# A bias table spread by one fp32 product, a later start for the third batch's v, and a new table of due times in an attention and feed-forward kernel

## The chip, the cores and the metric

The kernel runs on one core of one Trainium2 chip. The metric is the device time of one execution in microseconds (us). Before the change it is 368.13 us, the median of six runs (367.08 to 368.78).

The engines are named as in the profile: PE is TensorE (PEld its weight loads, which overlap its products), DVE is VectorE, ACT is ScalarE, POOL is GpSimd, SP is SyncE. SP, ACT and POOL issue the DMAs; the DMAs that POOL issues share one queue (q0 in the profile).

## The reference

Eight batches of eight heads of attention over 576 positions, head size 64, with an additive bias that depends on the distance of query and key, are followed by a feed-forward layer with a squared relu:

```
scores = q k^T / 8 + bias_table[bucket(|i - j|)]      # 32 buckets, 8 heads
attn   = softmax(scores);  x = attn v                 # -> 4608 tokens x 512
out    = (relu(x w_in)^2) w_out                       # w_in 512x2048, w_out 2048x512
```

From a distance of 128 on, the bucket is always the last, 31.

## The kernel before

**Attention.** A pair is two heads of one batch; there are 32 pairs, four to a batch. q and k of a pair are loaded (and cast to fp16 by the load), turned so that the head size lies on the partitions, multiplied into PSUM (`st`), raised to exponentials by ACT (`pt` for the first 512 keys, `pm` for the last 64), multiplied by the band of bias factors on DVE (L713), and multiplied by v (`va`, `vm`; L739, L746). For the pairs of batches 0 and 1 (0 to 7) PE turns q and k (L930); from batch 2 on DMA transposes that SP issues do it (L913). Batch 0 is worked in two halves (L812, L835, L857); the later batches whole (L974, L1025, L1000). The scores L812 and L974 use 64 rows of the array, all else 96 or 128.

**Bias.** Since the softmax does not change when one number is added to a whole row, the kernel uses exp(bias - bias of bucket 31), which is 1 from distance 128 on: only a band needs a factor. At the start it makes a table of these factors: `bt_sb` holds the bias table four times over (128 partitions x 8), by a load whose source has a first step of 0 (L376 to L380); `far_sb` holds the last row (L381); a product of a row of ones with `far_sb` (L402) puts that row on all 128 partitions; DVE subtracts (L408); ACT takes the exponential (`ex_sb`, L412); DVE spreads it over four selectors (`eb_sb`, L416); 96 products with one-hot columns (L429) and six copies (L441 on ACT, L443 on DVE) make the table `tb_sb`. It also makes `tm_sb` (L450).

**Feed-forward.** Tokens go in nine groups of 512. First layer: L1442 for group 0 (sixteen blocks of eight products: two halves of the tokens by eight blocks u of w_in; block u needs the piece u//2 of w_in), L1489 for the others, L1373 for parts of groups 7 and 8 in a scheme with seven products for eight. ACT takes the relu (L1452, L1518) and DVE the square. Second layer: L1218, the seven-product scheme with sums of `g` made on DVE (L1173) and sums of w_out made on DVE (L1148).

**Loads.** Issued by POOL in one queue: q and k of every pair, v of batches 0 and 1, w_in and w_out in four pieces each. POOL has eight slots (`r_lane`) for loads under way, so the ninth load is issued only when the first has landed. v of batches 2 to 7 is loaded as fp32 by SP into two rooms (`fs`) and cast by POOL (L630), five loads to a batch. For batch 2 these loads are held: POOL writes one column of each room (L602) and so the SP loads wait for it, and these two writes depend on the issue of the last piece of w_out (`i_wout[-1]`).

**What sets the order.** Every piece of work is an `Op` with costs on its possible engines, dependences, buffers and a due time. `Plan.schedule` walks through time: on each engine it takes, of the ops that can start first, the one with the smallest due time. The order found is written out and kept. `DUES` overwrites the due times of a few hundred ops by number; any change in the number of ops renumbers them.

Of the kernel before, what the change touches and what calls it, by code (L numbers as in the profile page):

```python
# [10 lines left out]
FP32 = mybir.dt.float32  # L11
FP16 = mybir.dt.float16
EXPF = mybir.ActivationFunctionType.Exp
# [5 lines left out]
B, H, S, D = 8, 8, 576, 64  # L19
NP = 4 * B  # L20
NBK = 32
# [20 lines left out]
V_EARLY, V_HW = 18900.0, 2  # L42
LATE2 = 7000
UNITS = {7: 1, 8: 2}
HALVES, HSTEP, HL1 = 1, 1650.0, (20000.0, 34000.0)

AT = (0, 0.5, 2, 2.5, 4, 5.5, 7)
# [15 lines left out]


DUES = """
8:-10082 18:14645 30:300187 31:89669 35:262867 36:167639 40:141372 70:12863 74:14200 76:7923 78:10303 80:10916
82:15510 86:16712 88:11688 90:22888 92:15486 98:18218 100:20325 102:18698 104:24117 106:22274 108:21955
110:20585 112:17720 114:22660 116:24333 118:24854 122:29293 124:30437 126:25266 128:33174 130:36581 132:40609
134:51257 136:44653 138:51581 140:48951 142:50028 144:58149 148:57611 150:61477 152:63431 154:61931 156:66311
158:66889 162:65338 164:65793 166:56376 168:67962 170:72120 172:69290 174:54109 176:67502 178:55993 196:79426  # L70
200:89582 204:93757 206:79008 208:72409 210:77212 214:73183 216:70645 218:79313 220:76603 222:85357 224:89011
226:93142 228:96877 232:85822 234:80876 238:92290 242:97174 244:85699 250:80035 259:178052 260:99215 262:99267
263:94523 265:102830 266:94655 268:90726 272:227849 274:97337 280:99383 284:102139 290:112200 294:119768
298:215875 300:111243 308:120928 316:292455 328:222317 340:120614 352:126648 372:290882 378:160123 388:315874
398:154756 400:154629 416:167698 428:163098 430:170467 446:157625 448:164616 474:193249 476:326588 532:43262
533:37155 566:352427 572:24133 585:21449 586:16465 587:204708 592:14599 602:18206 603:302815 606:16687 614:60883
624:23940 626:227369 635:24572 644:28677 645:32201 647:27594 652:32977 656:87863 662:27958 665:28412 667:205250
672:32876 673:30127 677:28664 678:35226 680:77471 688:28429 694:37858 696:40059 700:223775 702:35900 705:35909
708:53117 711:51743 714:57293 717:49012 723:57165 726:56821 729:45894 730:329911 732:52147 738:53922 741:160549
747:289501 748:55406 753:34997 766:39647 777:43315 780:28378 781:28998 794:190499 796:202913 801:53249 802:51377  # L80
808:35893 816:51696 822:366600 836:39718 838:41544 844:109201 849:53420 855:303647 858:55989 861:68919 874:85061
878:80108 894:83592 903:-31482 937:74470 948:83167 966:71026 967:67606 970:76116 972:74373 981:80209 995:78757
996:75913 997:79135 998:80070 999:81174 1013:88709 1034:85463 1045:100670 1048:345957 1050:105533 1063:95906
1087:126025 1091:130523 1094:105159 1096:130379 1100:125464 1107:123396 1110:104747 1111:120415 1116:126120
1120:119481 1123:112853 1128:107993 1136:132690 1140:133810 1143:114832 1147:125053 1150:33103 1151:132743
1158:127267 1161:133598 1178:111838 1183:122064 1212:107705 1215:110106 1220:108322 1231:116331 1243:107673
1244:132705 1249:136498 1250:141722 1252:138524 1266:154614 1279:137235 1290:170196 1295:139537 1309:155745
1313:157461 1318:142698 1320:168920 1324:178100 1338:169961 1342:165042 1347:151660 1349:165027 1353:178415
1360:154230 1363:160171 1364:172948 1367:167075 1371:182965 1374:172802 1377:182632 1379:188184 1382:183106
1393:150398 1396:136398 1398:139207 1407:162688 1439:159540 1442:165094 1444:160584 1457:156356 1462:162464  # L90
1476:171086 1494:178379 1496:95372 1513:192466 1517:206296 1522:201376 1526:211713 1533:196911 1537:195555
1542:191208 1546:222801 1551:200739 1554:200330 1555:209260 1558:35935 1562:223609 1566:193792 1573:210925
1577:216395 1580:214153 1584:204761 1587:221397 1611:179949 1617:185925 1632:157584 1638:187538 1643:188360
1673:204800 1678:201325 1684:208836 1735:235958 1746:247083 1749:236476 1753:241073 1755:232100 1758:46037
1759:255485 1762:69543 1764:28189 1767:246028 1768:258643 1775:224057 1779:236350 1786:235146 1790:231994
1793:247653 1797:260512 1800:225461 1819:215217 1833:222890 1851:236098 1856:236742 1859:216367 1883:242173
1886:229387 1888:224088 1897:252176 1943:260458 1947:277224 1948:272952 1952:266739 1959:262017 1963:176155
1968:269668 1972:265265 1981:279144 1988:265160 1992:64741 2003:269548 2010:73825 2013:261781 2032:291907
2035:289013 2037:286903 2040:293047 2064:272647 2065:274014 2069:249841 2083:15939 2096:275485 2104:257599
2111:304149 2133:278142 2142:287353 2147:290118 2158:278558 2181:2037 2182:291375 2189:39576 2193:314013  # L100
2198:26159 2207:312042 2222:313361 2229:315890 2233:58447 2240:320979 2243:310630 2258:242331 2260:323734
2267:332321 2280:282131 2283:327244 2285:319375 2290:184346 2296:334274 2333:323519 2354:325059
"""


# [156 lines left out]
def kernel(  # L262
# [10 lines left out]
    nc = tc.nc  # L273
    assert (_bucket(np.arange(128, S)) == NBK - 1).all()

    def io(ins):
        tc.keep_in_program_order(ins)
        return ins
# [3 lines left out]
        oh[i, _bucket(np.abs(252 + i - np.arange(512))), np.arange(512)] = 1.0  # L282
    oh_d = nc.inline_tensor(oh.reshape(128, 512), name="c_oh")
    sel = np.kron(np.eye(4), np.ones((NBK, H))).astype(np.float16)
    id_d = nc.inline_tensor(np.concatenate([np.eye(128, dtype=np.float16), sel], axis=1), name="c_id")

    single = ctx.enter_context(tc.tile_pool(name="single", bufs=1))
# [2 lines left out]
    def sb(name, shape, dtype=FP16):  # L290
        return single.tile(shape, dtype, name=name)
# [4 lines left out]
    w_out_sb = sb("w_out_sb", [128, 16, 512])  # L296
    tb_sb = sb("tb_sb", [128, H, 384])
    tm_sb = sb("tm_sb", [128, 4, 192])
    bt_sb = sb("bt_sb", [128, 8], FP32)
    far_sb = sb("far_sb", [1, 8], FP32)  # L300
    ex_sb = sb("ex_sb", [128, 8])
    eb_sb = sb("eb_sb", [128, 4, 8])
    stg = [[sb(f"{n}s{i}", [128, 12 * D]) for n in "qk"] for i in range(NSTG)]
# [13 lines left out]
    gs = [sb(f"g{i}", [128, 16, GT]) for i in range(NGB)]  # L317

    oh_sb = gs[0][:, 0, :]
    one_sb = gs[0].bitcast(FP32)[0:1, 2, 0:128]  # L320
    fs = [sb(f"f32{i}", [128, 512], FP32) for i in range(NF)]
    rts = [sb(f"rt{i}", [128, GT]) for i in range(NRT)]
    ys = [sb(f"y{i}", [128, 512], FP32) for i in range(NY)]
# [4 lines left out]
    g_ps = [psum.tile([128, 512], FP32, name=f"f{i}") for i in range(3)]  # L328

    P = Plan()  # L330
# [28 lines left out]
    def const(f):  # L359
        return lambda: f  # L360

    def load(*args, **kw):
        return loader(*args, **kw)[0]
# [3 lines left out]
    b_stg = [Buf(r_stg) for _ in range(4 * B)]  # L367
# [5 lines left out]
        for w, (n, e, t) in enumerate((("SP", nc.sync, q), ("ACT", nc.scalar, k)))  # L373
    ]
    l_id = load("SP", nc.sync, const(idsel_sb), const(id_d.ap()), (128, 27), due=-1)
    l_bt = load(  # L376
        "ACT", nc.scalar, const(bt_sb),
        const(bass.AP(tensor=bias_table.tensor, offset=bias_table.offset, ap=[[0, 4]] + [list(x) for x in bias_table.ap])),
        (128, 230), due=0,
    )  # L380
    l_far = load("ACT", nc.scalar, const(far_sb), const(bias_table[NBK - 1 : NBK, :]), (1, 27), due=1)  # L381
    l_oh = load("SP", nc.sync, const(oh_sb), const(oh_d.ap()), (128, 60), due=4)
    tabs = list(hw_specs.get_activation_tables(nc.m.arch))
    P.add(
# [10 lines left out]
        ),  # L395
        due=5,
    )
    z_one = P.add({"DVE": 141.0}, lambda: io(nc.vector.memset(one_sb, 1.0)), due=-2)
    far_b = Buf(r_g)
    o_far = P.add(  # L400
        {"PE": 250.0},
        lambda: io(nc.tensor.matmul(g_ps[far_b.slot][:, 0:8], one_sb, far_sb, start=True, stop=True)),  # L402
        [l_far, z_one], [far_b], 0.0, 0.0, "f",
    )
    o_bt = P.add(
        {"DVE": 150.0},
        lambda: io(
            nc.vector.tensor_tensor(out=bt_sb, in0=bt_sb, in1=g_ps[far_b.slot][:, 0:8], op=mybir.AluOpType.subtract)  # L408
        ),
        [l_bt, o_far], [far_b], -1.0,  # L410
    )
    o_ex = P.add({"ACT": 220.0}, lambda: io(nc.scalar.activation(out=ex_sb, in_=bt_sb, func=EXPF)), [o_bt])  # L412
    o_eb = P.add(
        {"DVE": 230.0},
        lambda: io(
# [89 lines left out]
    def pdue():  # L505
        pool_due[0] += 1.0
        return pool_due[0]
# [21 lines left out]
    def load_rows(p, w):  # L529

        b, hp = divmod(p, 4)
        src = (q, k)[w][b, 2 * hp : 2 * hp + 2]
        l_qk[p, w] = [
            load(
                "POOL", nc.gpsimd,
                lambda e=e: rows(stg[b_stg[p].slot][w])[:, 0:4, ds(64 * e, D)],
                const(src[e, 0:512, :].rearrange("(t p) d -> p t d", p=128)),
                (512, 14.5), s_fix, [b_stg[p]], pdue(),
            )
            for e in range(2)  # L540
        ] + [
            load(
                "POOL", nc.gpsimd,
                lambda: stg[b_stg[p].slot][w][0:64, 512:640].rearrange("p (e d) -> p e d", e=2),
                const(src[:, 512:S, :].rearrange("e p d -> p e d")),
                (128, 14.5), s_fix, [b_stg[p]], pdue(),
            )
        ]

    def cast_first(w):  # L550

# [39 lines left out]
        load_v_tail(b)  # L591

    r_f = Ring(NF, True)

    def load_v_fp32(b):

# [2 lines left out]
        if b == V_HW:  # L599

            held = [
                P.add({"POOL": 60.0}, lambda t=t: io(nc.gpsimd.memset(t[:, 0:1], 0.0)), [i_wout[-1]], (), due)  # L602
                for t in fs
            ]
        for tt in range(5):
# [991 lines left out]
```

## Time and profile before

| | |
|---|---|
| median of six runs | 368.13 us (367.08 to 368.78) |
| the profiled execution's own time | 368.39 us |
| its span, first to last instruction | 366.6 us, so 1.8 us lie around it |
| PE busy | 354.6 us, 97% of the span |
| DVE, ACT, POOL busy | 271.5, 263.1, 186.1 us |
| DMA | 44.28 MB, mean 121 GB/s |
| granted PE clock | 1.00 over nearly the whole span |

The page gives each engine's busy time, then the span in 40 slices with busy tenths. The waits tell which engine waited for whom; the timeline lists instructions with start, duration, engine, line, tiles and, in brackets, the idle time before them. A landing time below is the issue's start in the timeline plus the issue-to-landing time of the DMA list. For the loads around the weights that gives, numbered in the order of the queue: second piece of w_in 33.1 (issued 25.2, 7.9 to landing), a k, the fourth piece of v of batch 1 at 34.7 (26.6 + 8.1), first piece of w_out 38.3, a k, second of w_out 42.1, third of w_in 45.5, third of w_out 48.8 (30.3 + 18.5), fourth of w_in 52.2, fourth of w_out 54.9. The first two loads of v of batch 2 are issued by SP at 35.8 and 36.3 and land 11.9 and 18.0 us later.

### The profile page before, as it was taken

To read this page: it belongs to the slowest core of one execution; us is meant where nothing else is said; L and a number is where in the kernel's file an instruction comes from. 1 tells how busy PE (TensorE), PEld (TensorE's weight loads), DVE (VectorE), ACT (ScalarE), POOL (GpSimd) and SP (SyncE) were. 2 spreads that over 40 slices of the span, in tenths; PEclk is the share of its full clock that TensorE was granted. 3 is DMA by queue.
4 is the path that set the end of the run, shared out by engine and by line. 5 is a ranking of instruction groups with operands and counts; after the bars stand their busy time and mean duration, and the time that the engine had idled before them with its cause. 6 is when DMAs were issued, how large, how long until landed. Compare 5 with 4: busy or idle time off the path is not lost.

```text
span 366.6 us, 10230 instructions
## 1 busy us (share of the span) xinstructions
PE 354.6 (97%) x4062; PEld 253.5 (69%) x4062; DVE 271.5 (74%) x622; ACT 263.1 (72%) x390; POOL 186.1 (51%) x342
## 2 busy tenths in 40 slices
PE   4998999999999999999999999999999999999996
PEld 2767787866378546877776666476667786787785
DVE  3798899957885679477597588756688885787673
ACT  5999998479975888678986778967778434725620
POOL 7987529989999977888777772021000000000000
PEclk9999999999999999999999999999999999999999
DMA  9999999999999999999999996143200232020132
GB/s 162 132 156 175 199 172 121 157 184 181 157 137 160 185 160 188 160 164 168 167 116 161 174 150 99 30 108 84 75 3 13 60 84 64 2 89 0 35 111 88
DMA packets 162294, 44.28 MB, mean 121 GB/s; under 512 B 145734, under 2 KB 162246, under 8 KB 162246
## 3 DMA queue, kind: packets, MB, share of 16 engines
q0 software_dynamic: 74208, 14.53, 52.1%
q1 hardware_dynamic: 87696, 28.80, 43.2%
q8 instruction: 32, 0.52, 0.6%
q10 hardware_dynamic: 342, 0.30, 0.3%
q14 instruction: 16, 0.13, 0.1%
HBM read 36.88 MB, written 9.44 MB: 126 GB/s over the span
## 4 chain that ended last, share of the span: by engine, by line
PE 80%; DMA 7%; DVE 6%; POOL 3%; ACT 2%; issue 1%; POOLq 0%
PE f L1218 27%; PE f L1489 27%; PE pv L746 8%; PE st L974 7%; DMA w_out_sb<-in_moe_w_out_dram 3%; PE pv L739 2%; DMA w_in_sb<-in_moe_w_in_dram 2%; PE f L1442 2%; DMA qs<-in_q_dram 2%; PE st L1025 2%; DVE pt L713 2%; PE st L1000 1%; DVE s L1173 1%; PE st L1373 1%; POOL va L346 1%
## 5 line engine op out<-in xcount | busy, mean ns | idle before, releaser
L987 ACT ACTIVATE pt<-st 128x1024 f16<-128x1024 f32 x112 | 108.8, 1029 | 27.1 <-PE st L974 26.5
L1489 PE MATMUL f<-xt,w_in_sb 128*128 128x512 f16 (+4 forms) x592 | 111.8, 333 | 0.0
L1518 ACT ACTIVATE rt<-f 128x512 f16<-128x512 f32 x116 | 67.8, 607 | 25.8 <-PE f L1489 24.4
L1489 PEld LDWEIGHTS <-w_in_sb 128*128 128x128 f16 x592 | 51.7, 98 | 43.4 <-issue 9.3
L713 DVE TENSOR_TENSOR pt<-pt,tb_sb 128x512 f16<-128x512 f16 (+3 forms) x108 | 62.0, 593 | 12.7 <-ACT pt L987 11.8
L1528 DVE TENSOR_TENSOR g<-rt 128x512 f16<-128x512 f16 x116 | 49.9, 437 | 23.4 <-ACT rt L1518 22.0
L1218 PEld LDWEIGHTS <-g 128*128 128x128 f16 x576 | 54.4, 98 | 9.2 <-issue 2.5
L346 POOL DMA_DIRECT2D ks<-in_k_dram x79 | 55.6, 713 | 6.7 <-DMA w_out_sb<-in_moe_w_out_dram 4.3
L346 POOL DMA_DIRECT2D qs<-in_q_dram x79 | 55.3, 709 | 7.2 <-DMA w_in_sb<-in_moe_w_in_dram 2.8
L746 PE MATMUL pv<-va,pt 128*128 128x65 f16 x1280 | 55.0, 193 | 0.2 <-DVE pt L713 0.2
L746 PEld LDWEIGHTS <-pt 128*128 128x128 f16 x1280 | 50.3, 97 | 2.5 <-DVE pt L713 0.4
L1218 PEld LDWEIGHTS <-s 128*128 128x128 f16 x432 | 41.5, 98 | 8.3 <-issue 2.1
L1246 DVE SCALAR_TENSOR_TENSOR y<-f,y 128x512 f32<-128x512 f32 (+1 forms) x47 | 31.3, 667 | 19.4 <-PE f L1218 16.7
L1218 PE MATMUL f<-wt,g 128*128 128x256 f16 x288 | 36.4, 273 | 0.0
L1218 PE MATMUL f<-w_out_sb,s 128*128 128x256 f16 x288 | 36.2, 273 | 0.0
L739 PE MATMUL pv<-vm,pm 128*128 128x130 f16 x160 | 35.4, 221 | 0.1
L974 PE MATMUL st<-qt,kt 64*128 64x512 f16 x224 | 33.9, 381 | 0.0
L957 POOL COPY qz<-qt 64x64 f16<-64x64 f16 x54 | 18.6, 345 | 29.9 <-DMA qt<-qs 12.6
L1218 PE MATMUL f<-w_out_sb,g 128*128 128x256 f16 x272 | 33.6, 273 | 0.0
L765 DVE TENSOR_TENSOR x<-pv,r 128x384 f16<-128x384 f32 (+1 forms) x64 | 31.2, 488 | 1.3
L1173 DVE TENSOR_TENSOR s<-g,s 128x1024 f16<-128x1024 f16 x36 | 24.8, 692 | 0.2
L760 DVE RECIPROCAL r<-pv 128x6 f32<-128x6 f32 (+1 forms) x64 | 11.9, 186 | 16.9 <-PE pv L746 16.2
(104 smaller groups left out, 422.4 us busy)
## 6 DMA issues: line engine op xcount, KB each, us to landing
out_dram<-y SPq DMA_DIRECT2D x34, 256.0 KB, 2.7
f<-in_v_dram SPq DMA_DIRECT2D x24, 256.0 KB, 5.8
qs<-in_q_dram POOLq DMA_DIRECT2D x48, 64.0 KB, 4.9
ks<-in_k_dram POOLq DMA_DIRECT2D x48, 64.0 KB, 4.6
w_in_sb<-in_moe_w_in_dram POOLq DMA_DIRECT2D x4, 512.0 KB, 11.9
w_out_sb<-in_moe_w_out_dram POOLq DMA_DIRECT2D x4, 512.0 KB, 15.9
qs<-in_q_dram POOLq DMA_DIRECT2D x7, 144.0 KB, 5.1
ks<-in_k_dram POOLq DMA_DIRECT2D x7, 144.0 KB, 5.6
```

Source lines behind the costliest of these rows:

```text
L346: lambda: io(eng.dma_start(out=out_(), in_=in_())),
L713: io(nc.vector.tensor_tensor(out=a, in0=a, in1=t, op=MULT))
L739: nc.tensor.matmul(ps[:, i, :, :], pm[:, c : c + 128], vm[:, hp, :, 0:65], start=True, stop=False)
L746: nc.tensor.matmul(ps[:, i, e, :], pt[:, (2 * jt + e) * S + c : (2 * jt + e) * S + c + 128], va[:, jt, 2 * hp + e, 0:65], start=False, sto ...
L765: nc.vector.tensor_tensor(out=xs[xb.slot][:, qt0 : qt0 + nq, :].rearrange("p t (e d) -> p t e d", e=2), in0=ps[:, :, :, 0:64], in1=rs[rb.s ...
L974: nc.tensor.matmul(sets_ps[st.slot][:, e, :], kt[rw, ts(jt, 128)], qt[rw, 0:512], start=True, stop=True,)
L987: nc.scalar.activation(out=p5(pts[pb.slot])[:, jt, :, 0:512], in_=sets_ps[st.slot], func=EXPF, scale=SCALE)
L1218: nc.tensor.matmul(home[bf.slot][:, ts(s_, HALF)], left(c, s_), right(c), start=(c == 0 and (s_ == 0 or apart) and (own or i not in before ...
L1246: nc.vector.scalar_tensor_tensor(out=dst, in0=ps, scalar=OSC, in1=ys[y[plus].slot][:, cs], op0=MULT, op1=mybir.AluOpType.add,)
L1489: nc.tensor.matmul(g_ps[bank.slot][:, a:z], w_in_sb[:, kk, ts(nt, 128)], xt_sb[:, kk, c : c + z - a], start=(kk == 0), stop=(kk == 3),)
L1518: io(nc.scalar.activation(out=rts[rb.slot], in_=g_ps[bank.slot], func=RELUF))
L1528: nc.vector.tensor_tensor(out=gs[gb1.slot][:, nt, :], in0=rts[rb.slot], in1=rts[rb.slot], op=MULT)
```

## The change

1. The bias table is loaded once, 32 partitions x 8, and the load of its last row goes. A constant `c_rep` (32 x 128, fp32: the identity four times side by side, less 1 in its last row) is loaded in its stead. One fp32 product of the two, over 32 rows, gives on 128 partitions bias - bias of bucket 31; ACT takes the exponential straight from PSUM. The row of ones, the fp32 product over one row and the DVE subtraction go. Both new loads lie in `g0`, in places that `g` uses only later.
2. The two POOL writes that hold v of batch 2 depend on the last issue of pair 8's k (`i_qk[8, 1]`) in place of the last issue of w_out.
3. `DUES` is new throughout. With it the order of all engines changes.

```diff
-8:-10082 18:14645 30:300187 31:89669 35:262867 36:167639 40:141372 70:12863 74:14200 76:7923 78:10303 80:10916
...
+0:6314 10:217026 16:13035 20:13348 21:258484 25:16976 56:-3806 60:10549 64:7807 66:10391 72:10797 74:9599
...
+V_AFTER = 8
...
+    rep = np.tile(np.eye(NBK, dtype=np.float32), (1, 4))
+    rep[NBK - 1] -= 1.0
+    rep_d = nc.inline_tensor(rep, name="c_rep")
...
-    one_sb = gs[0].bitcast(FP32)[0:1, 2, 0:128]
+    rep_sb, bt_sb = (gs[0].bitcast(FP32)[0:NBK, 2 + i, 0:n] for i, n in enumerate((128, H)))
...
-    l_bt = load(
-        "ACT", nc.scalar, const(bt_sb),
-        const(bass.AP(tensor=bias_table.tensor, offset=bias_table.offset, ap=[[0, 4]] + [list(x) for x in bias_table.ap])),
-        (128, 230), due=0,
-    )
-    l_far = load("ACT", nc.scalar, const(far_sb), const(bias_table[NBK - 1 : NBK, :]), (1, 27), due=1)
+    l_bt = load("ACT", nc.scalar, const(bt_sb), const(bias_table), (NBK, 230), due=0)
+    l_rep = load("ACT", nc.scalar, const(rep_sb), const(rep_d.ap()), (NBK, 40), due=1)
...
-    z_one = P.add({"DVE": 141.0}, lambda: io(nc.vector.memset(one_sb, 1.0)), due=-2)
...
     o_far = P.add(
-        {"PE": 250.0},
-        lambda: io(nc.tensor.matmul(g_ps[far_b.slot][:, 0:8], one_sb, far_sb, start=True, stop=True)),
-        [l_far, z_one], [far_b], 0.0, 0.0, "f",
+        {"PE": 560.0},
+        lambda: io(nc.tensor.matmul(g_ps[far_b.slot][:, 0:8], rep_sb, bt_sb, start=True, stop=True)),
+        [l_bt, l_rep], [far_b], 0.0, 0.0, "f",
     )
-    o_bt = P.add(
-        {"DVE": 150.0},
-        lambda: io(
-            nc.vector.tensor_tensor(out=bt_sb, in0=bt_sb, in1=g_ps[far_b.slot][:, 0:8], op=mybir.AluOpType.subtract)
-        ),
-        [l_bt, o_far], [far_b], -1.0,
+    o_ex = P.add(
+        {"ACT": 220.0},
+        lambda: io(nc.scalar.activation(out=ex_sb, in_=g_ps[far_b.slot][:, 0:8], func=EXPF)),
+        [o_far], [far_b],
     )
-    o_ex = P.add({"ACT": 220.0}, lambda: io(nc.scalar.activation(out=ex_sb, in_=bt_sb, func=EXPF)), [o_bt])
...
-                P.add({"POOL": 60.0}, lambda t=t: io(nc.gpsimd.memset(t[:, 0:1], 0.0)), [i_wout[-1]], (), due)
+                P.add({"POOL": 60.0}, lambda t=t: io(nc.gpsimd.memset(t[:, 0:1], 0.0)), [i_qk[V_AFTER, 1]], (), due)
```

The order that results, as far as the prediction uses it. SP issues the constants before the first q, ACT issues the first k as its first load. The cast of the first q moves from ACT to DVE. PE begins with the turns of pair 0's k, then the fp32 product, then pair 0's q, pair 1's k, the first sixteen products of the table, pair 1's q, and only then the first scores. The loads of POOL before the second piece of w_in are the same in number and size; after it come two k, the first piece of w_out, the third of w_in, two pieces of w_out, the fourth piece of v of batch 1, the fourth piece of w_in, the fourth of w_out. The two writes that hold v of batch 2 stand thirteen entries later, behind eight loads of pairs 8 to 10.

## Prediction

> **What bounds the kernel now.** First the busy times and the busy tenths of the page: PE is the engine to watch.
>
> ```profile
> PE 354.6 (97%) x4062; PEld 253.5 (69%) x4062; DVE 271.5 (74%) x622; ACT 263.1 (72%) x390; POOL 186.1 (51%) x342
> ```
>
> Then the busy times by stretch (columns: length, then busy us and count for PE, PEld, DVE, ACT, POOL, then granted clock, DMA share, GB/s), which tell where PE's idle time lies:
>
> ```profile
> 0.00:5.00 5.00, 0.57 (x4) 0.51 (x4) 2.33 (x13) 2.13 (x2) 3.89 (x10) 1.00 0.66 161
> 5.00:10.00 5.00, 4.00 (x58) 2.67 (x59) 1.06 (x7) 3.98 (x8) 4.11 (x8) 1.00 1.58 162
> 10.00:20.00 10.00, 8.66 (x208) 6.25 (x208) 8.09 (x25) 9.86 (x17) 9.22 (x16) 1.00 1.28 134
> 20.00:30.00 10.00, 9.50 (x185) 6.83 (x182) 9.39 (x30) 10.00 (x16) 9.06 (x14) 1.00 1.51 153
> 30.00:40.00 10.00, 8.85 (x152) 6.75 (x149) 7.04 (x25) 9.04 (x15) 6.40 (x21) 1.00 1.33 194
> 40.00:50.00 10.00, 9.83 (x140) 8.05 (x138) 9.74 (x28) 9.15 (x14) 4.80 (x8) 1.00 1.22 196
> 50.00:100.00 50.00, 49.76 (x550) 33.74 (x549) 41.22 (x89) 40.24 (x61) 43.76 (x74) 1.00 1.60 159
> 100.00:200.00 100.00, 99.91 (x1176) 71.41 (x1176) 72.83 (x159) 78.27 (x112) 85.25 (x153) 1.00 1.50 161
> ```
>
> From 50 us on PE is idle for 0.3 us in 150, later for nothing; before 50 us it is idle 8.6 us, 5.4 of them in the first 10. Between 10 and 30 us ACT is full (19.86 of 20). So after 50 us the time is PE's work; only the first 50 us can give anything back. Last the waits of PE between 4 and 60 us and the timeline at the two places that matter below:
>
> ```profile
> PE f L930 <- ACT qs L555: 2.4, 1, 2.4
> PE f L930 <- DMA ks<-in_k_dram: 1.0, 1, 1.0
> PE f L835 <- POOL qz L957: 0.8, 1, 0.8
> ...
> 33.85 0.45 PE L930 MATMUL f<-id_sb,ks 96*64 96x96 f16 x12 [0.98 <-DMA ks<-in_k_dram]
> ...
> 42.93 0.22 PE L739 MATMUL pv<-vm,pm 128*128 128x130 f16 x1
> ```
>
> The first wait is the start itself (first data, first cast). The one at 33.85 is for the k of a pair of batch 1. At 42.93 the first values of pair 4 begin: eight us after the last piece of their v landed (34.7), so that load is far from the path now.
>
> **Work after 50 us.** The change leaves PE's products the same in kind and number but for the fp32 one. Each visit to the 64-row scores costs PE a turn there and back: after L974 the next group starts 0.54 us later (34.48 to 35.02) where 2 x 0.21 would do. In the built order those turns number 112 before and after for L974, so this term is 0. For the early L812 they go from 24 to 28: two more visits, at some 0.15 to 0.3 us a turn **+0.6** (0 if they fall into ACT's full stretch, 1.2 at most).
>
> **The first 10 us.** This is the old chain of the table in the timeline:
>
> ```profile
> 2.06 0.56 PE L402 MATMUL f<-far_sb,g 1*128 1x8 f32 x2 [2.06 <-DMA far_sb<-in_bias_table_dram]
> 4.10 0.84 ACT L555 ACTIVATE qs<-g 96x768 f16<-96x768 f32 x1 [0.46 <-DMA g<-in_q_dram]
> 5.22 0.84 ACT L555 ACTIVATE ks<-g 96x768 f16<-96x768 f32 x1 [0.28 <-DMA g<-in_k_dram]
> 8.82 0.16 DVE L408 TENSOR_TENSOR bt_sb<-bt_sb,f 128x8 f32<-128x8 f32 x1
> 9.51 0.20 ACT L412 ACTIVATE ex_sb<-bt_sb 128x8 f16<-128x8 f32 x1
> 9.75 0.18 DVE L416 TENSOR_TENSOR eb_sb<-id_sb,ex_sb 128x32 f16<-128x32 f16 x1 [0.77 <-ACT ex_sb L412]
> ```
>
> L408 (0.16) and the memset (0.17) go; both lay in idle DVE time (3.4 of 10 us busy), so they give 0. The load of 128 rows of 32 B goes: 4 KB among 2.27 MB of the first 15 us, 0 in transfer, and its 0.64 us of issue on ACT ended at 2.3, before ACT's first cast could start; its successor takes as long or less. Now the k is issued at 0.74 as q was, so it should land at 4.1 and be cast on ACT to 4.9; its turns on PE run 5.0 to 5.7 (0.69 each, as the row of L930 at 4.99 has it). The fp32 product comes next; the trace shows it over one row only, 0.56. Over 32 rows I take 0.56 (0.35 if only one of the two passes counts, 1.4 if like a turn of twelve it doubles). PE then waits for the q cast, now on DVE: no such cast is in the trace; the nearest DVE row, fp32 from PSUM, 128x512 (L443), is 0.645, so 0.97 for 768, and fp16 rows at 0.44 per 512 give 0.65. I take 0.8: q lands at 5.2, is cast by 6.0, while the fp32 product ends at 6.3. Exponential 6.5, selectors 6.9, table products from about 8.0, two us before the old 9.97. But the order puts these ahead of the first scores: pair 0's go from 7.94 to about 9.2 and ACT's first big exponential from 8.60 to about 10.3. Early table, late scores: by 10 us PE has done 48 turns either way. **0** (-0.4 to +0.8).
>
> The Trainium skill has a rule on this cast, "VectorE: DVE Perf Modes": a copy with one fp32 source in SBUF runs at twice the rate, as it takes both read ports. By it the cast would be about 0.45 us, an estimate from the page's rates; no row here shows it, and the sum stays the same since the fp32 product ends later anyway.
>
> **ACT's full stretch, 10 to 34 us.** Up to the last exponential of batch 0 ACT loses the q cast (0.84), two turned copies (2 x 0.6) and one table copy (0.62), 2.6 us; it gains 1.5 to 2.2 of idle time before 16 us, as its exponentials start late and wait for table products between them. **-0.4** (-1.1 to +0.3).
>
> **The wait at 33.85.** In the new order three turns stand together, but five further L1442 blocks, one more turn of twelve, and one more half of scores stand ahead of pair 4's values. PE reaches the awaited k later than it lands (33.8): **-1.0** (0 if the pair before it is late).
>
> **What is late next: v of batch 1.** Its fourth piece now lies behind two k, three pieces of w_out and one of w_in. Those are just the loads that before landed between 33.1 and 48.8, so by those rows it lands at 48.8. PE comes to it 5 x 0.87 + 0.54 + 0.45 = 5.4 us later than 42.93, that is at 48.3, and less the gains above and plus the extra turns (-0.8) at 47.5. So there is a wait where there was none, 1.3 us at most by these rows. It is less if holding v of batch 2 speeds up the weights. The rows are against it: the second piece of w_in, with no SP load beside it, took 3.6 us of the queue (29.5 to 33.1), the second of w_out and third of w_in, with one beside, 3.1 and 3.4. The transfers before 56 us show 18% of 16 engines for the SP side, which is some 2 us by 48.8. I take a wait of **+0.6**, between landing at 47.4 (0) and, at 3.6 a piece, 49.9 (+2.4).
>
> The page "DMA: Bandwidth & Descriptors" (section "Issuing engines are not separate DMA queues") says that all issuers' transfers run on the same 16 engines and interleave. By it, the 0.5 MB held back would bring the piece forward by those 2 us, the wait would be 0 and the sum 0.6 lower. The rows of the pieces speak against it, and the measured one decides.
>
> **v of batch 2.** It begins to land around 59 in place of 47.7. Behind the two POOL writes stands all of POOL's queue, but they wait only for an issue on POOL itself: 0. The five loads and casts end near 72 (before: last cast 68.6 to 69.0). In the built order the first values of pair 8 lie 7 us of PE work later than before (83.3), so 18 us are left: cover of 14 before, 18 after. **0.**
>
> **Sum.** +0.6 + 0 - 0.4 - 1.0 + 0.6 = -0.2; against the profiled execution 368.4 - 0.2 = 368.2. That one lies 0.26 over the median of the runs shown, so **367.9**. Within 0.3% (1.1 us, about what a measurement of this kernel can tell from no change) is the likeliest.
>
> **The rivals.** *Faster:* the held v does free the queue, the piece of v is there by 47.4 (the 0.6 goes), the extra turns are covered (another 0.6), ACT loses no time between table products (0.4): -1.8, 366.3. For it: the wait at 33.85 and 2.6 us less on ACT. Against it: ACT's later first exponential. *Slower, by one mechanism:* v of batch 1 lands at 49.9, PE waits 2.4 at the first values of pair 4: -0.8 + 2.4 = +1.6, 369.7. It decides once the piece lands after 48.3; the fourth w_in (52.2, needed near 52.7 by the thirteenth L1442 block) would then press too. *The order itself:* new due times bring waits after 50 us, where the old order has 0.3; twice 1 us of idle PE would make 370. *The change does not do what it says:* table and hold are off the path, and the old time stays, 368.1, inside the first case.
>
> **How the numbers follow.** No change 0.40, faster 0.32, late v 0.20, waits after 50 us 0.08. The range takes the faster case (366.3, down to 366.0 if the first 10 us give 0.3) and the late v (369.7), and leaves out the rest: 366.0 to 370.0. The likeliest case alone: 367.0 to 369.2. Chances: faster 0.32, same 0.40, slower 0.28.
>
> **What would show it.** First table products near 8 us and first L812 near 9.2; no PE wait on a k near 34; a PE idle before the first L739 of pair 4, near 48, released by the load of `va`; PE idle under 0.5 us from 50 us on; L630 casts done by 73. Wrong if PE idles elsewhere after 50 us, or if the pieces of weights land over 2 us earlier.

## The result and the profile after

The changed kernel takes 366.12 us (median of 22 runs, 365.03 to 369.06), beside 368.28 us for the kernel before in the same rounds. The ratio is 0.9946, with a 95% interval of 0.9932 to 0.996: faster by 0.5%. That lies inside the range on record (366.0 to 370.0), but it is the rival's time ("faster", 366.3) and not the forecast's (367.9). Measured once more (`after_again` below), the same kernel gave 0.9973 (0.9958 to 0.9988). So the gain is 0.3 to 0.5%, and two measurements of one kernel can differ by 0.003.

Line numbers in the changed kernel are a few lower: L746 is now L743, L739 L736, L930 L927, L812 L809, L822 L819, L974 L971, L1442 L1439, L402 L401, L429 L425.

Busy times of the changed kernel by stretch, with columns as in the prediction's table (length, busy us and count for PE, PEld, DVE, ACT, POOL, granted clock, DMA share, GB/s):

```profile
0.00:5.00 5.00, 0.00 (x0) 0.00 (x0) 2.15 (x12) 1.83 (x2) 3.90 (x10) 1.00 0.61 154
5.00:10.00 5.00, 4.03 (x71) 3.17 (x72) 2.17 (x7) 2.84 (x6) 4.31 (x8) 1.00 1.59 171
10.00:20.00 10.00, 8.96 (x208) 6.36 (x207) 8.83 (x26) 9.79 (x16) 9.27 (x16) 1.00 1.31 136
20.00:30.00 10.00, 9.12 (x179) 6.77 (x176) 9.22 (x29) 10.00 (x15) 8.98 (x15) 1.00 1.57 167
30.00:40.00 10.00, 9.75 (x172) 7.88 (x169) 8.96 (x29) 8.96 (x16) 7.09 (x22) 1.00 1.23 200
40.00:50.00 10.00, 10.00 (x134) 8.03 (x132) 8.99 (x27) 9.59 (x16) 4.49 (x7) 1.00 1.53 192
50.00:100.00 50.00, 50.00 (x571) 33.92 (x569) 42.08 (x93) 40.11 (x59) 47.10 (x84) 1.00 1.57 163
```

From 30 to 50 us PE was idle for 1.32 us before; now for 0.25. From 50 to 100 us it was idle for 0.24; now for nothing. Between 10 and 30 us ACT is as full as it was (19.79 of 20, before 19.86). PE's busy time itself fell too, from 354.6 to 352.7 us, with 4062 products in both profiles.

The new table chain, in the timeline of the changed kernel:

```profile
4.45 0.84 ACT L551 ACTIVATE ks<-g 96x768 f16<-96x768 f32 x1 [1.02 <-DMA g<-in_k_dram]
5.34 0.69 PE L927 MATMUL f<-id_sb,ks 96*64 96x96 f16 x12 [5.34 <-ACT ks L551]
5.46 0.56 DVE L553 CAST qs<-g 96x768 f16<-96x768 f32 x1 [2.19 <-DMA g<-in_q_dram]
6.66 0.56 PE L401 MATMUL f<-g 32*128 32x8 f32 x2 [0.63 <-DMA g<-c_rep]
8.25 0.61 PE L425 MATMUL f<-eb_sb,g 128*128 128x32 f16 x16
```

The fp32 product takes 0.56 us over 32 rows as it did over one. But it waits 0.63 us for the constant, which lands at 6.5 us, and the turns of q stand behind it. The table's products begin at 8.25 (before 9.97), the first scores at 9.41 (before 7.94).

Then the place where PE waited for the k of a batch-1 pair, and the place where the prediction feared a wait for v of batch 1, both in PE's timeline of the changed kernel:

```profile
34.45 0.45 PE L927 MATMUL f<-id_sb,qs 96*64 96x96 f16 x12
34.73 0.68 PE L927 MATMUL f<-id_sb,ks 96*64 96x96 f16 x24
...
46.40 0.39 PE L997 MATMUL st<-qz,kt 128*128 128x128 f16 x4
46.63 0.22 PE L736 MATMUL pv<-vm,pm 128*128 128x130 f16 x1
46.69 0.41 PE L743 MATMUL pv<-va,pt 128*128 128x65 f16 x8
```

No idle time stands in brackets in either place. The two k landed at 32.7 and 33.4, the fourth piece of v of batch 1 at 44.8, and PE reached the values that need it at 46.6.

Why was the piece there so early? Here is the DMA between 24 and 46 us (share is the time that a queue's packets took, as a share of the span of 16 engines), first of the changed kernel:

```profile
DMA packets 7292, 4.17 MB, mean 190 GB/s; under 512 B 3542, under 2 KB 7287, under 8 KB 7287
## 3 DMA queue, kind: packets, MB, share of 16 engines
q0 software_dynamic: 7287, 4.10, 135.6%
```

and then of the run `hold_undone` below, which is the changed kernel but loads v of batch 2 early, as before:

```profile
DMA packets 8657, 4.15 MB, mean 189 GB/s; under 512 B 5467, under 2 KB 8651, under 8 KB 8651
## 3 DMA queue, kind: packets, MB, share of 16 engines
q0 software_dynamic: 6634, 3.57, 118.0%
q1 hardware_dynamic: 2017, 0.51, 17.6%
```

The sum is the same, 4.17 and 4.15 MB at 190 and 189 GB/s. The 0.51 MB that SP's queue (q1) moves is taken from POOL's queue (q0).

### The profile page after: what moved, and what is told of

Its sections match the earlier page's. It is cut to its first block, busy times and chain, and to the rows that moved or that the text cites. A ratio compares the mean times of both kernels' runs of the same rounds, so it can differ in the third digit from the quotient of the medians.

```text
span 363.9 us, 10232 instructions
## 1 busy us (share of the span) xinstructions
PE 352.7 (97%) x4062; PEld 252.8 (69%) x4062; DVE 269.9 (74%) x622; ACT 260.2 (72%) x385; POOL 185.4 (51%) x345
## 4 chain that ended last, share of the span: by engine, by line
PE 92%; ACT 3%; DMA 1%; DVE 1%; issue 0%; ACTq 0%
PE f L1215 30%; PE f L1486 28%; PE pv L743 10%; PE st L971 8%; PE f L1439 4%; PE pv L736 3%; ACT pt L819 2%; PE st L1022 2%; PE st L997 2%; PE st L1370 1%; DMA g<-c_rep 1%; PE f L927 1%; PE pv L1370 1%; ACT pt L864 1%; PE f L1089 1%; PE st L809 0%
## 5 line engine op out<-in xcount | busy, mean ns | idle before, releaser
L1486 PE MATMUL f<-xt,w_in_sb 128*128 128x512 f16 (+4 forms) x592 | 113.7, 333 | 0.0
L743 PE MATMUL pv<-va,pt 128*128 128x65 f16 x1280 | 54.6, 193 | 0.0
L743 PEld LDWEIGHTS <-pt 128*128 128x128 f16 x1280 | 50.2, 97 | 2.0
L736 PE MATMUL pv<-vm,pm 128*128 128x130 f16 x160 | 35.4, 221 | 0.1
L971 PE MATMUL st<-qt,kt 64*128 64x512 f16 x224 | 33.9, 381 | 0.0
L1170 DVE TENSOR_TENSOR s<-g,s 128x1024 f16<-128x1024 f16 x36 | 24.8, 694 | 0.1
L757 DVE RECIPROCAL r<-pv 128x6 f32<-128x6 f32 (+1 forms) x64 | 11.8, 184 | 14.8 <-PE pv L743 14.6
```

What stands on the lines that cost most here:

```text
L736: nc.tensor.matmul(ps[:, i, :, :], pm[:, c : c + 128], vm[:, hp, :, 0:65], start=True, stop=False)
L743: nc.tensor.matmul(ps[:, i, e, :], pt[:, (2 * jt + e) * S + c : (2 * jt + e) * S + c + 128], va[:, jt, 2 * hp + e, 0:65], start=False, sto ...
L971: nc.tensor.matmul(sets_ps[st.slot][:, e, :], kt[rw, ts(jt, 128)], qt[rw, 0:512], start=True, stop=True,)
L1486: nc.tensor.matmul(g_ps[bank.slot][:, a:z], w_in_sb[:, kk, ts(nt, 128)], xt_sb[:, kk, c : c + z - a], start=(kk == 0), stop=(kk == 3),)
```

## The experiments

Two theories at the start. **A:** the gain has parts that can be told apart, namely the k that no longer comes late (about 1 us) and the held v, which frees the DMA engines for the weights. **B:** the new order as a whole brings it, and table and hold are off the path. Each expectation names its own A and B (and C) for its run. In the edits, `move(ops, to)` takes ops out of the order that was computed and puts them behind (or, with `before`, ahead of) another; everything else stays. Kernels that were run together are judged by the ratio to the kernel before in the same rounds; there its median was 367.65 to 367.89 us.

| run | order | us | ratio to before | 95% interval |
|---|---|---|---|---|
| hold_undone | new | 366.51 | 0.9967 | 0.9948 to 0.9987 |
| new_order_old_table | new | 366.06 | 0.9950 | 0.9931 to 0.9969 |
| product_after_q | new | 365.87 | 0.9956 | 0.9939 to 0.9974 |
| rep_first | new | 365.85 | 0.9956 | 0.9936 to 0.9976 |
| q5_early | new | 366.95 | 0.9973 | 0.9949 to 0.9998 |
| rep_and_product | new | 365.52 | 0.9951 | 0.9933 to 0.9969 |
| after_again | new | 366.46 | 0.9973 | 0.9958 to 0.9988 |
| old_order_hold | old | 367.48 | 0.9996 | 0.9973 to 1.0019 |
| old_order_table | old | 368.20 | 1.0008 | 0.9986 to 1.0029 |
| old_order_k_early | old | 367.55 | 1.0007 | 0.9986 to 1.0029 |
| old_order_hold_k | old | 367.37 | 0.9999 | 0.9978 to 1.0021 |
| old_order_k_dve | old | 368.07 | 1.0007 | 0.9988 to 1.0027 |

**The hold, undone in the new order (`hold_undone`).**

```diff
+    move(holds, max(i_wout, key=order.index))
```

> The changed kernel with one edit: the two writes that hold v of batch 2 stand right behind the issue of the last piece of w_out, as before, so its loads start near 35 us again. Theory A, the held v frees the 16 shared DMA engines: the pieces of w_in and w_out take 3.1 to 3.4 us each again in place of 2.5 to 2.7, the fourth piece of v of batch 1 lands near 47 to 48.8 in place of 44.8, PE waits 0.5 to 1.5 us for it at the first values of pair 4, and the time is 366.6 to 368. Theory B, the gain is the order's alone and the hold is off the path: no wait, 365.8 to 366.4. If the pieces take 2.5 to 2.7 us with v of batch 2 beside them, A is wrong in its mechanism too.

Measured: 0.9967. The pieces of weights behind the first piece of w_out took 2.82, 2.90, 3.53, 2.85 and 2.53 us (2.99, 2.52, 2.68, 2.58 and 2.52 in the changed kernel), and the last landed 17.1 us after the first instead of 14.0. The piece of v landed at 46.10. PE's timeline there shows no bracket, but the first `va` product began 0.26 us after the `vm` product ahead of it, against 0.06 in the changed kernel, so some 0.2 us were lost (L738 and L745 are this run's numbers for L736 and L743):

```profile
45.88 0.22 PE L738 MATMUL pv<-vm,pm 128*128 128x130 f16 x1
46.14 0.40 PE L745 MATMUL pv<-va,pt 128*128 128x65 f16 x8
```

So the mechanism of A is right (SP's loads slow POOL's), but its price of 0.5 to 1.5 us is not. The median, 366.51, lies between the ranges of the two theories. The ratio 0.9967 lies between the changed kernel's 0.9946 and 0.9973, so no difference is shown. In this one profiled execution the queue ran ahead: the second piece of w_in landed at 30.4, in the changed kernel at 32.0. The price in other executions may be higher than 0.2.

**The hold alone, in the old order (`old_order_hold`).**

```diff
+    move(holds + i_v2, k8[-2])      # k8: the three issues of pair 8's k
```

> The kernel before, its own order, with only the hold moved: v of batch 2 waits for the next-to-last load of k of pair 8. Theory A: the pieces of the weights take 2.5 to 2.7 us in place of 3.1 to 3.4 and land up to 5 us sooner near 50, but in the old order nothing on PE waits for them (v of batch 1 landed at 34.7 already), so the time stays at 368.0 to 368.6. Theory B, the hold alone brings the gain: 366.1 to 367.3. The wait for the k of a batch-1 pair near 33.85 stays in both, about 1 us.

Measured: 0.9996, no change, as A expected (in us, 367.48 lies between the two ranges; the kernel before had 367.89 in these rounds). From the first to the last piece of w_out 14.6 us passed (before 16.7). PE still waited 0.7 us for the k. By the ratio the hold alone gains nothing.

**The table, undone in the new order and alone in the old one (`new_order_old_table`, `old_order_table`).**

```diff
-        lambda: io(nc.tensor.matmul(g_ps[far_b.slot][:, 0:8], rep_sb, bt_sb, start=True, stop=True)),
+        lambda: io(nc.tensor.matmul(g_ps[far_b.slot][:, 0:8], one_sb, far_sb, start=True, stop=True)),
...
+            io(nc.vector.tensor_tensor(out=bt_sb, in0=bt_sb, in1=g_ps[far_b.slot][:, 0:8], op=mybir.AluOpType.subtract)),
```

That is the core of the first, with the old loads and the row of ones. The second is the other way round, with the product behind the turns of pair 1's q.

> The changed kernel with the old table chain: broadcast load of 128 rows, far row, memset, product over one row, subtraction. Theory A, the table chain is off the path, since ACT is full from 10 to 34 us and the turns of q are late anyway: 365.8 to 366.5. Theory B, the new product costs, because PE waits 0.63 us for the constant before it: the old chain is up to 0.6 us faster. Theory C, the new chain brings part of the gain: 366.5 to 367.2.

> The kernel before, its own order, with only the new table chain: one fp32 product of the 32-row table with a constant, the exponential read from its result, no memset, no subtraction, no broadcast load. Theory A: the table chain is off the path in the old order too, 367.9 to 368.6. Theory C, the shorter chain alone brings 0.3 to 1 us: 367.2 to 368.0.

Measured: 0.9950 and 1.0008. No worth of the table chain is shown in either order. In the old order it even put off the first big exponential, from 8.60 to 9.83, and nothing of that was left at the end.

**The late k, undone in the old order (`old_order_k_early`).**

```diff
+    w2 = sorted((l.deps[0] for l in l_win), key=order.index)[1]
+    move([l_qk[5, 1][0].deps[0]], w2, before=True)
```

> The kernel before, its own order, with only the first load of k of pair 5 issued ahead of the second piece of w_in, so that it lands some 3 us before PE asks for it at 33.85. Theory A, the wait of about 1 us there lies on PE's path and goes one for one: 367.1 to 367.5. Theory B, ACT, full from 10 to 34 us, or the next load takes its place: 367.9 to 368.4.

Measured: 1.0007, so theory A fell. The wait at 33.85 was gone, and the time did not move. Theory B named ACT or the next load as what takes its place; PE's timeline of this run shows another engine:

```profile
60.54 0.60 PE L974 MATMUL st<-qt,kt 64*128 64x512 f16 x4
61.72 0.22 PE L739 MATMUL pv<-vm,pm 128*128 128x130 f16 x1 [0.58 <-DVE x L765]
...
68.25 0.39 PE L746 MATMUL pv<-va,pt 128*128 128x65 f16 x7 [0.20 <-DVE pt L713]
...
69.16 0.61 PE L974 MATMUL st<-qt,kt 64*128 64x512 f16 x4
```

PE now waits for VectorE, to free a PSUM room (L765) and for a product with the bias (L713). VectorE's own work at that place:

```profile
59.16 0.68 DVE L1173 TENSOR_TENSOR s<-g 128x1024 f16<-128x1024 f16 x1
59.76 0.18 DVE L760 RECIPROCAL r<-pv 128x6 f32<-128x6 f32 x1
59.87 1.33 DVE L1173 TENSOR_TENSOR s<-g,s 128x1024 f16<-128x1024 f16 x1
61.12 0.54 DVE L765 TENSOR_TENSOR x<-pv,r 128x384 f16<-128x384 f32 x1
```

The division of L765 stands behind a sum that took 1.33 us here; in most rows such a sum takes 0.65 to 0.77. The extra 0.6 is as long as PE's wait of 0.58, so in this execution that one slow sum may be the whole of that wait.

Busy times by stretch show that VectorE was as full in the kernel before. First the kernel before:

```profile
50.00:55.00 5.00, 5.00 (x76) 4.21 (x75) 4.28 (x13) 4.73 (x9) 0.76 (x1) 1.00 1.49 152
55.00:60.00 5.00, 5.00 (x52) 3.41 (x50) 5.00 (x13) 4.69 (x9) 4.78 (x7) 1.00 0.78 94
60.00:65.00 5.00, 5.00 (x77) 4.08 (x77) 5.00 (x9) 4.18 (x6) 5.00 (x9) 1.00 1.31 138
65.00:70.00 5.00, 4.76 (x48) 3.96 (x46) 5.00 (x10) 1.17 (x3) 4.90 (x9) 1.00 1.38 152
```

then `old_order_k_early`:

```profile
55.00:60.00 5.00, 5.00 (x64) 3.95 (x62) 5.00 (x12) 4.70 (x7) 5.00 (x8) 1.00 1.25 165
60.00:65.00 5.00, 4.42 (x53) 3.40 (x51) 5.00 (x9) 3.02 (x4) 4.94 (x8) 1.00 2.52 127
```

and the changed kernel:

```profile
50.00:55.00 5.00, 5.00 (x49) 4.22 (x48) 5.00 (x13) 4.71 (x9) 4.75 (x9) 1.00 1.30 158
55.00:60.00 5.00, 5.00 (x76) 3.79 (x73) 4.99 (x11) 4.14 (x6) 4.96 (x9) 1.00 1.73 180
60.00:65.00 5.00, 5.00 (x46) 3.94 (x45) 4.97 (x10) 3.06 (x4) 5.00 (x8) 1.00 1.67 135
65.00:70.00 5.00, 5.00 (x76) 3.67 (x75) 3.90 (x9) 2.40 (x3) 4.74 (x11) 1.00 1.91 180
```

The third pair of numbers behind the length is VectorE's. In the kernel before it is full from 55 to 70 us; with k early it is just as full from 55 to 65, and PE loses 0.58 us from 60 to 65. In the new order VectorE is full from 50 to 65, and PE runs through without a gap.

**Two and two (`old_order_hold_k`, `old_order_k_dve`).** The first joins the two moves above. The second joins the early k with

```diff
+    for i in range(11, 14):
+        move([nor[i]], rec[i])      # the division L765 right behind its reciprocal L760
```

> The kernel before, its own order, with two edits at once: the hold of v of batch 2 behind k of pair 8, and the first load of k of pair 5 ahead of the second piece of w_in. Alone the first gave 367.48 (ratio 0.9996) and the second 367.55 (1.0007). Theory A, each takes away one of two limits that stand behind each other (the wait for k near 33, and VectorE's full stretch from 55 to 67 us, where in the second run PE waited 0.85 and 0.36 us again): together 366.0 to 366.8, most of the whole change. Theory B, VectorE's full stretch is due to the old order itself and not to v of batch 2: PE waits near 61 and 68 as in the second run, 367.2 to 367.9.

> The kernel before with the first load of k of pair 5 early, and, on VectorE, the division of the values by their sums (L765) put straight behind the reciprocal (L760) for the twelfth to fourteenth visit, ahead of the sums L1173 that stood between. In the run with k early alone PE waited 0.85 us near 60.8 for that division and 0.36 near 67.9 for a product with the bias. Theory A, the place of the one instruction in VectorE's queue makes the wait: it goes, and the time falls to 366.5 to 367.0. Theory B, VectorE is full from 55 to 67 us, so that what is moved back (L1173, the bias products L713) becomes late and PE waits there: 367.3 to 367.9.

Measured: 0.9999 and 1.0007; in both runs theory A's number failed. In `old_order_k_dve` the wait for L765 is gone, and PE waits 0.44 us at 65.04 for a sum that had been put back (`f<-wt,s`, released by s of L1173). That is what theory B expected of a full VectorE. `old_order_hold_k` has no wait of PE from 50 to 80 us in its profile, where theory B expected two, and still no gain in its times. So a wait for VectorE does not explain this run; what does stays open.

How VectorE's full stretch passes a lead on can be read from the starts of the sixth, eighth and ninth visit to the scores of 64 rows (L974) in the old order, where PE does the same work between them in all six kernels:

| old order | sixth | eighth | ninth | span |
|---|---|---|---|---|
| before | 56.09 | 62.65 | 70.82 | 366.6 |
| old_order_table | 55.48 | 62.61 | 71.00 | 366.7 |
| old_order_hold_k | 55.04 | 61.59 | 69.25 | 365.1 |
| old_order_hold | 54.94 | 61.49 | 69.17 | 364.8 |
| old_order_k_dve | 54.55 | 61.10 | 69.33 | 365.0 |
| old_order_k_early | 53.87 | 60.54 | 69.16 | 365.8 |

However early PE comes to the sixth visit (53.87 to 55.04 in the lower four rows), it does not come to the ninth before 69.16. From the sixth to the ninth it takes 14.2 us in `old_order_hold` and `old_order_hold_k`, 14.8 in `old_order_k_dve` and 15.3 in `old_order_k_early`: a lead of up to a microsecond is lost in VectorE's full stretch. More than that the table does not show. The kernel before is 1.5 to 1.7 us later than these four at the ninth visit, yet its times are not shown to be longer than theirs. Each row is a single execution: those of `old_order_hold`, `old_order_hold_k` and `old_order_k_dve` took 366.55, 366.92 and 366.85, which is 0.4 to 1.2 us less than the medians of these kernels.

**The first ten microseconds (`product_after_q`, `rep_first`, `rep_and_product`).**

```diff
+    move([o_far], turns[0, 0])                           # product_after_q
+    move([l_rep.deps[0]], l_bt.deps[0], before=True)     # rep_first; rep_and_product has both
```

> The changed kernel with the fp32 product of the table behind the turns of q of pair 0, so that PE doesn't wait 0.63 us for the constant ahead of them. Theory A, the first microseconds lie on the path: 0.3 to 0.6 us faster, 365.5 to 365.8. Theory B, ACT's full stretch from 10 us on takes it back, or the table products come later: 365.9 to 366.4.

> The changed kernel with the load of the constant issued ahead of the load of the bias table, so that the later of the two lands sooner: in the changed kernel the table landed at 4.91 and the constant at 6.52. Theory A, the constant's 32 rows of 512 bytes are the slow ones and an earlier issue brings them near 6.0: up to 0.6 us faster, 365.5 to 366.0. Theory B, whichever of the two is second lands near 6.5, or ACT's full stretch hides the gain: 365.9 to 366.4.

> The changed kernel with two edits that alone gave 365.85 and 365.87 against 366.12: the constant loaded ahead of the bias table, and the fp32 product behind the turns of q of pair 0. Theory A, both ease PE's first 10 us, and the gains add: 365.4 to 365.7. Theory B, both differences were noise, as ACT is full from 10 us on: the same as the changed kernel in these rounds, to 0.2 us.

Measured: 0.9956, 0.9956 and 0.9951. In the first two the table products began at 8.21 and 8.28 instead of 8.25, so neither edit moved anything behind it. `rep_and_product` has the lowest median of all (365.52 from 6 runs; 366.46 for the changed kernel in the same rounds). That lies in theory A's range, and the 0.9 us between the two are more than B's 0.2; but the two intervals overlap (0.9933 to 0.9969, and 0.9958 to 0.9988). No version is shown to be faster than the changed kernel, and for this one it is not ruled out.

**One load earlier (`q5_early`).**

```diff
+    move([q5], pool[pool.index(q5) - 1], before=True)    # first q of pair 5, ahead of a v piece
```

> The changed kernel with the first load of q of pair 5 issued one place earlier, ahead of a piece of v of batch 1. Theory A, the idle time of PE at 23.86 (0.77 us, of which 0.6 is put down to that load) lies on the path: 365.4 to 365.7. Theory B, ACT is full from 20 to 30 us and PE would wait for it a little later: 365.9 to 366.4.

Measured: 0.9973, no gain; the median lies above both ranges. PE's idle times between 22 and 36 us in this run:

```profile
23.25 0.39 PE L809 MATMUL st<-qt,kt 64*128 64x256 f16 x4 [0.16 <-ACT pt L819]
25.90 0.39 PE L809 MATMUL st<-qt,kt 64*128 64x256 f16 x4 [0.52 <-ACT pt L819]
32.41 0.38 PE L997 MATMUL st<-qz,kt 128*128 128x128 f16 x4 [0.68 <-POOL qz L954]
33.43 1.05 PE L1439 MATMUL f<-xt,w_in_sb 128*128 128x256 f16 x8 [0.64 <-DMA w_in_sb<-in_moe_w_in_dram]
```

The wait for q at 23.91 (0.55 in the changed kernel) is gone; 0.52 of waiting for an exponential stands two microseconds later. That is what theory B expected, with ACT as the bound there. The 0.64 at 33.43 is a piece of w_in that landed at 33.4, 1.4 us later than in the changed kernel; in this execution all of the queue ran later from 20 us on, so it is not shown that the edit caused it.

**The changed kernel again (`after_again`).**

> The changed kernel as it is, beside the other three on the same chip: a ratio of 0.994 to 0.996 to the kernel before is expected. By how far it differs from the first time shows what two runs of one kernel can differ by.

Measured: 0.9973, above what was expected. The first measurement gave 0.9946.

**What follows.** All eight measurements of the new order (seven kernels, the changed one twice) have ratios of 0.9946 to 0.9973, all five edited kernels with the old order 0.9996 to 1.0008, whatever table, hold or single load they have. The gain is the order's. Table and hold were not undone together in the new order, nor joined in the old one. By the profiled executions (single ones, of kernels that differ a little, spans scattering by 0.7 us):

| mean over the profiled executions | old order (6) | new order (8) | difference |
|---|---|---|---|
| span | 365.67 | 364.05 | -1.6 |
| PE busy, of the whole span | 354.2 | 352.9 | -1.3 |
| end of the last big exponential of batch 0 on ACT (L822, L819) | 31.53 | 31.18 | -0.35 |
| PE idle 32 to 50 us | 0.40 | 0.15 | -0.25 |
| PE idle 50 to 80 us | 0.44 | 0.00 | -0.44 |
| PE idle 80 to 360 us | 0.17 | 0.11 | -0.06 |

Listed idle time is the smaller part: over the whole span it falls by 0.3, PE's busy time by 1.3. All fourteen profiles have 4062 products, and each of the eight (352.6 to 353.4) is less busy than each of the six (353.6 to 354.8). Busy time holds delays between products that overlap, such as the 0.2 us before the `va` product of `hold_undone`, which no bracket shows. To see where they went, count for each product the median step from a product of its shape to the next one; what the clock has gone beyond the sum of these steps is PE's lag. In the new order the lag is smaller by 0.1 us at 32 us, 0.7 at 50, 1.35 at 80 and 1.6 from 200 us on, by the means of these executions. So ACT's earlier end brings little by itself. Most is won between 32 and 80 us, and half of that from 50 us on, where VectorE's full stretch lies. Which moves of the new order do it was not tried.

## Why the prediction was right in its range and wrong in its likeliest case

**First 10 us, 0: right.** k landed at 4.43 (4.1 said), q's cast on DVE took 0.56 (0.8 taken; 0.45 was the prediction's estimate from the rate that the Trainium skill gives in "VectorE: DVE Perf Modes", 0.11 below the row), the table products came at 8.25 (8.0), the first L809 at 9.41 (9.2). The wait of 0.63 for the constant was not foreseen, and the runs that were to ease it or go round it show no gain.

**ACT's full stretch, -0.4: right.** First to last big exponential of batch 0 took 22.8 us before (8.60 to 31.40) and 20.5 after (10.66 to 31.13). So 2.3 us of other work left ACT (2.6 said), its start is 2.1 later (1.5 to 2.2 of added idle time said), and it ends 0.27 earlier; over all profiles 0.35.

**Extra turns, +0.6: mis-sized.** The bound of 0 held. They lie before 28.5 us, in ACT's full stretch, and that ended no later for them.

**v of batch 1, a wait of +0.6: the step that failed.** There is no wait. The prediction weighed the section "Issuing engines are not separate DMA queues" of the Trainium skill's "DMA: Bandwidth & Descriptors" against rows of single pieces, and chose the rows. The runs agree with the rule: with 0.51 MB of SP's loads beside them POOL's pieces took 2.5 to 3.5 us, without them 2.5 to 3.0, at one and the same total rate. From the landing of the second piece of w_in to that of this piece of v 15.7 us passed with the hold undone, just what the prediction took from its rows (33.1 to 48.8), and 12.8 in the changed kernel. So the hold was worth 2.9 us of the queue, where the prediction's rows gave it nothing. One of the prediction's own signs of being wrong came with it: the last piece of w_out landed at 49.9, and not at 54.9. The row that was chosen, 3.6 for the second piece of w_in with nothing of SP's beside it, is no price: the same piece took 3.8 in the changed kernel, 2.6 in `old_order_table` and 2.5 in `hold_undone`. A single row of one execution was too weak to set against it. The piece landed at 44.8 instead of 48.8. With the hold undone it landed at 46.1, and PE lost some 0.2 us to it: in these two executions the hold is cover more than gain.

**v of batch 2, 0: right.** Its first load landed at 54.3 (59 said), its last cast ended at 73.0 (72 said), and no product waited for it.

**The wait at 33.85, -1.0: right in size, wrong in its reason.** It is gone, as said. But it was counted one for one, and in the old order its removal shows no gain (1.0007). It was also read off one execution: PE waited 0.98 us there in the kernel before, 0.7 in `old_order_hold`, and not at all in `old_order_table`, which differs in the table alone. The sentence "after 50 us the time is PE's work; only the first 50 us can give anything back" is the fault behind it: the profile before shows VectorE at 5.00 of 5.00 in three slices from 55 to 70 us, and 0.24 us of PE idle just there. That was a second bound with almost no room, and the prediction read it as none. In `old_order_k_early` it took back part of the lead (0.58 and 0.20 us of waiting); that it took all of it, in this run and the others, is not shown.

**Work after 50 us, 0: mis-sized.** PE idle from 50 us on goes from 0.33 to 0.02 in the two profiles, and from 0.61 to 0.11 in the means; with the delays inside busy time, PE's lag falls by 0.9 from 50 us on. The prediction took the work of PE as fixed, since the products are the same in kind and number; PE's busy time fell by 1.3. The new order has VectorE's stretch five microseconds earlier, and PE does not wait in it in any of the eight profiles. That this is what lets the other gains reach the end is our reading; it was not tested by itself.

So the sum was too high by 0.6 for the turns, 0.6 for the wait and 0.3 to 0.5 of idle time after 50 us (0.9 of lag); the rival "faster" had the first two and 0.4 on ACT. That the rival's 366.3 comes within 0.2 us of the result is luck in part: it too counts the wait at 33.85 one for one and has nothing after 50 us. The result lies only 0.12 us above the lower end of the range, which was set by the rival.

## What to carry to other kernels

A wait on the busiest engine need not be worth its length: look in the slices behind it for another engine at 10 tenths, and do not count the gain before it is seen to pass that stretch. When parts of a change show no worth by themselves, in both directions, the gain may be the order's; run each part in the old order and undo each in the new one before it is given credit. A held load made the others land sooner here, but that is time only where something waits for them. And compare busy times too: delays between overlapping instructions are listed nowhere as idle.

## What the runs showed of the hardware

**The third load of ACT's queue lands late, whatever its size.** In the changed kernel the bias table (32 rows of 32 bytes) issued at 1.18 landed at 4.91, and the constant (32 rows of 512 bytes) issued at 1.68 landed at 6.52. With the two exchanged (`rep_first`), the constant landed at 4.96 and the table at 6.55. So for these two loads the place in the queue sets the time, and not the bytes. The third load scatters: 5.9 to 7.0 in the other kernels with the new order and the new table.

**A VectorE sum waits for a POOL cast or copy that is already running.** The sum `s<-g,s` of two fp16 tiles of 1024 (L1173 before, L1170 after) took 0.66 to 0.72 us in all 126 cases of five profiles (before, `old_order_hold`, `old_order_k_early`, after, `hold_undone`) in which no POOL cast or copy ran beside it. Of the 54 with one beside, 23 began while one was running that went on for another 0.16 us or more. Of these, 22 ended 0.54 to 0.55 us after it had ended, so that they took 0.71 to 1.11 us; one, the 1.33 at 59.87 above, ended 0.90 after. Of the 17 that began ahead of the cast or copy, 15 took 0.65 to 0.69 and two took 0.98 and 1.09. The Trainium skill ("SBUF — State Buffer", "Terms") says that VectorE and GpSimd share one pair of ports under an exclusive lock, so that the loser is blocked; these rows agree, and nearly always the sum was the loser where the other was there first.
